# Windowed attention and an expert layer on one core: the second product of the last two chunks in seven products for eight

## The chip, the core and the metric

One of the eight cores of a Trainium2 chip runs one program. Its engines work side by side, each in the order of its own program: TensorE (PE; its weight loads are shown as PEld), VectorE (DVE), ScalarE (ACT), GpSimd (POOL), and SyncE (SP), which issues nearly all DMAs here. The metric is the device time of one execution in microseconds (us). Lower is better.

## The reference, cut to what matters

```python
scores = scale * q @ k.T                   # 8 x 8 heads, 576 positions, 64 wide; half the heads with a
attn = softmax(where(mask, scores, -1e9))  # window of 32, half with a dilated one
x = (attn @ v) as [4608, 512]
h = x @ w_in                               # w_in 512 x 2048
sp = maximum(h, 0) + log1p(exp(-abs(h)))   # softplus
g = h * erf(sp)
out = g @ w_out                            # w_out 2048 x 512
```

The inputs are float32 (the weights reach the chip as the bits of float64). A product of two float32 matrices is made of three TensorE products: each operand is split into a high part, which TensorE's fp32r format holds, and a low part, the rest; hi*hi + hi*lo + lo*hi is summed in PSUM.

## The kernel before

**Chunks.** The 4608 tokens are nine chunks of 512. The attention is worked off in small units between the matmuls of the first chunks, and its output x is kept turned, features on partitions. Three chunks (`PAIRED`) go through both products in the plain way: `mm1` (line 511) makes h, `mm2` (line 630) multiplies g with w_out. The other six are three pairs (`DOUBLES`), and the h of a pair is made by Strassen's algorithm: seven products for eight over two halves of the 512 features, two halves of a block d of 256 hidden columns, and the two chunks A and B. The sums of x (`big_load`, `big_less`, `big_hi`, `big_lo`) and of w_in (`build`, kept in DRAM as `ws`) are made ahead; `load_left` (line 576) brings the seven left operands of each d, in two DMAs.

**One d of a pair.** `mm1_big(d, k)` (761) is product k, six matmuls of 128x128 by 128x512 into one of two PSUM banks, `h` and `tx`. `take_big(d, k)` (771) adds it on VectorE to the sums that become h of A and of B, 128x1024 each. `argument_big` (798) is softplus on ScalarE: for A after take 4, for B after take 6. Erf needs another table of ScalarE; it runs in the next period (877), then `multiply_big` (803) makes g on VectorE. The g of B is stored to DRAM (`kept_g`), and `load_g` (810) brings it back when its turn comes; the g of A stays in SBUF.

**Periods.** `period(i, late)` (837) writes out the order of the work. Each period multiplies one item, the g of one chunk for one d, with w_out: 24 matmuls of 128x128 by 128x512 (`item_products`, 821; `mm`, 635), in four quarters of six, into four accumulators of 512 tokens by 512 columns. `split_item` (817) cuts g into its parts one period ahead. Eight of a pair's sixteen periods also hold the 42 matmuls of an h, in four groups between the quarters. So the items run behind h: with the last pair, d=16 to 23, periods 32 and 33 still multiply the last g of the pair before, periods 34 to 39 start the pair's A, and ten more periods without h end the program with the last of A and all of B.

**Order.** Nothing is rearranged: under `manual_schedule` every engine has its instructions in the order in which the code emits them, and waits on semaphores for what it needs. SP is one queue too. `AFT` lists small jobs by period and quarter, among them those that prepare the next pair. A tile name has a fixed number of buffers (`rows` 4, `w` 4, `hc`, `s`, `ghi`, `glo` 2, `v0`, `v1`, `qk0`, `qk1`, `o` 1); who takes one waits until its last readers are done, DMAs among them.

Of the kernel before, what the change touches and what calls it, by code (L numbers as in the profile page):

```python
# [139 lines left out]
def attn_moe_kernel(ctx: ExitStack, tc: tile.TileContext, qk, v, masks, eye, w_in, w_out, out):  # L140
# [518 lines left out]
    def store(c):  # L659
        last = c == NCH - 1  # L660
        for tt in range(TOK // P):
# [83 lines left out]
    for k in range(1, DOUBLES):  # L745
# [14 lines left out]

    def mm1_big(d, k):
        bank_ = (h, bank)[(7 * d + k) % 2]
        name = ORDER[k]
        w = left(NT + d).rearrange("p (b i c n) -> p b i c n", b=len(LEFT), i=2, c=2)[:, LEFT.index(name)]
        x = big[RIGHT[LEFT.index(name)]]
        for c in range(2):
            for n, (wi, xi) in enumerate(((0, 0), (0, 1), (1, 0))):
                nc.tensor.matmul(bank_, w[:, wi, c, :], x[c][:, xi, :],  # L768
                                 start=(c == 0 and n == 0), stop=(c == 1 and n == 2))

    def take_big(d, k):
        y = (h, bank)[(7 * d + k) % 2]
        if k == 0:
# [2 lines left out]
        add = lambda out, to: nc.vector.tensor_tensor(out=out, in0=y, in1=to, op=ALU.add)  # L776
        if k == 0:
            nc.vector.tensor_copy(out=a[:, 1], in_=y)  # L778
        elif k == 1:
            add(a[:, 0], a[:, 1])  # L780
        elif k == 2:
            add(b[:, 0], a[:, 1])
        elif k == 3:
            add(b[:, 1], b[:, 0])
        elif k == 4:
            add(a[:, 1], b[:, 1])
        elif k == 5:
            nc.vector.tensor_tensor(out=b, in0=y.rearrange("p (j n) -> p j n", j=1).broadcast_to([P, PAIR, TOK]),
                                    in1=b, op=ALU.add)
# [13 lines left out]
    def multiply_big(kind_, d):  # L803
        e = hs[kind_, d]
        nc.vector.tensor_tensor(out=e, in0=e, in1=ls[kind_, d], op=ALU.mult)
# [319 lines left out]
```

## Time and profile before

| | |
|---|---|
| three runs | 892.3, 893.34, 897.2 us, median 893.34 |
| the profiled execution | 892.89 us, span 890.9 us |
| busy, of the span | PE 871.2, PEld 700.1, DVE 633.6, ACT 564.5, POOL 81.3 us |
| first product of d=18 | at 743.06 us |
| last matmul | starts at 886.99 us |

The profile shows one execution. A row of a group of instructions has the line, engine, operation, what it writes<-reads, the shape, the count, then busy time and mean ns of one, and the idle time ahead of it with what ended it. A row of the timeline or of the chain of waits has its start and its length in us first; equal neighbours are merged (x6). Matmuls overlap in the pipeline, so one lasts longer than the step from start to start.

### The profile page before, as it was taken

To read this page: it belongs to the slowest core of one execution; us is meant where nothing else is said; L and a number is where in the kernel's file an instruction comes from. 1 tells how busy PE (TensorE), PEld (TensorE's weight loads), DVE (VectorE), ACT (ScalarE), POOL (GpSimd) and SP (SyncE) were. 2 spreads that over 40 slices of the span, in tenths; PEclk is the share of its full clock that TensorE was granted. 3 is DMA by queue.
4 is the path that set the end of the run, shared out by engine and by line. 5 is a ranking of instruction groups with operands and counts; after the bars stand their busy time and mean duration, and the time that the engine had idled before them with its cause. 6 is when DMAs were issued, how large, how long until landed. Compare 5 with 4: busy or idle time off the path is not lost.

```text
span 890.9 us, 20870 instructions
## 1 busy us (share of the span) xinstructions
PE 871.2 (98%) x8134; PEld 700.1 (79%) x8134; DVE 633.6 (71%) x1575; ACT 564.5 (63%) x1271; POOL 81.3 (9%) x97
## 2 busy tenths in 40 slices
PE   7799999999999999999999999999999999999998
PEld 3367888888888888788887778888888888888886
DVE  5878888987798889777676765666566647576622
ACT  6889888897788886675677442774445434445321
POOL 2312201111111110011000000010000000000000
PEclk9999999999999999999999999999999999999999
DMA  8874446464658896566675741674449125442341
GB/s 272 295 245 154 128 155 197 148 232 127 222 203 270 295 341 248 172 224 221 204 239 200 272 176 54 209 237 161 166 155 361 51 83 200 166 154 83 140 144 48
DMA packets 66915, 170.41 MB, mean 191 GB/s; under 512 B 7680, under 2 KB 14592, under 8 KB 63744
## 3 DMA queue, kind: packets, MB, share of 16 engines
q1 hardware_dynamic: 66528, 168.55, 55.1%
q8 instruction: 64, 1.05, 0.5%
q10 hardware_dynamic: 288, 0.52, 0.2%
q14 instruction: 35, 0.29, 0.1%
HBM read 122.91 MB, written 46.14 MB: 190 GB/s over the span
## 4 chain that ended last, share of the span: by engine, by line
PE 91%; DVE 5%; DMA 1%; ACT 1%; issue 1%; POOL 1%; SPq 0%; DVEq 0%; POOLq 0%; ACTq 0%
PE acc L636 43%; PE h L768 13%; PE tx L768 13%; PE h L521 7%; PE tx L521 7%; PE sp L275 3%; PE sp L217 3%; PE sp L256 1%; PE h L357 1%; DMA qk<-in_qk_dram 1%; DMA v<-in_v_dram 1%; DVE w L458 0%; DVE w L459 0%; DVE prob L228 0%; DVE win L453 0%
## 5 line engine op out<-in xcount | busy, mean ns | idle before, releaser
L636 PE MATMUL acc<-wout_hi,ghi 128*128 128x512 f32 x576 | 227.4, 395 | 0.5 <-DVE ghi L611 0.4
L636 PE MATMUL acc<-wout_lo,ghi 128*128 128x512 f32 x576 | 224.6, 390 | 0.0
L636 PE MATMUL acc<-wout_hi,glo 128*128 128x512 f32 x576 | 159.0, 389 | 0.0
L636 PEld LDWEIGHTS acc<-wout_hi,ghi 128*128 128x128 f32 x576 | 108.2, 188 | 23.3 <-DVE ghi L611 0.9
L636 PEld LDWEIGHTS acc<-wout_hi,glo 128*128 128x128 f32 x576 | 108.1, 188 | 22.8
L636 PEld LDWEIGHTS acc<-wout_lo,ghi 128*128 128x128 f32 x576 | 108.2, 188 | 21.7
L251 POOL TENSOR_TENSOR prob<-prob,rinv 128x256 f32<-128x256 f32 x72 | 72.7, 1016 | 477.0 <-DVE ssum L249 239.9
L238 ACT ACTIVATE prob<-prob,nmax 128x64 f32<-128x64 f32 x288 | 96.3, 338 | 10.5 <-DVE nmax L228 10.3
L801 ACT ACT_TABLE_LOAD x24 | 30.8, 1283 | 93.0 <-DVE dbl L776 47.3
L768 PE MATMUL tx<-win 128*128 128x512 f32 x288 | 74.1, 392 | 0.8 <-DVE hc L778 0.8
L228 DVE CUSTOM_DVE_ANT_0 prob<-sp,cst 128x64 f32<-128x64 f32 x288 | 45.3, 220 | 40.6 <-ACT rows L317 28.2
L768 PE MATMUL h<-win 128*128 128x512 f32 x288 | 74.0, 392 | 0.0
L768 PEld LDWEIGHTS tx<-win 128*128 128x128 f32 x288 | 53.5, 188 | 12.7 <-DVE hc L778 1.2
L768 PEld LDWEIGHTS h<-win 128*128 128x128 f32 x288 | 53.4, 188 | 12.0 <-DVE dbl L778 0.8
L612 DVE TENSOR_TENSOR glo<-hc,ghi 128x512 fp32r<-128x512 f32 x50 | 34.5, 692 | 33.4 <-PE acc L636 22.6
L238 ACT ACTIVATION_READ_ACCUMULATOR prob<-prob,nmax 128x1 f32 x288 | 54.7, 190 | 0.0
L612 DVE TENSOR_TENSOR glo<-dbl,ghi 128x512 fp32r<-128x512 f32 x48 | 33.4, 696 | 28.3 <-PE acc L636 15.6
L521 PE MATMUL h<-x,win 128*128 128x512 f32 x192 | 48.8, 396 | 0.0
L877 ACT ACTIVATE s<-s 128x1024 f32<-128x1024 f32 x48 | 48.2, 1052 | 0.3
L521 PE MATMUL tx<-x,win 128*128 128x512 f32 x192 | 48.0, 392 | 0.0
L801 ACT ACTIVATE s<-hc 128x1024 f32<-128x1024 f32 x24 | 25.5, 1061 | 34.9 <-DVE hc L776 22.8
L611 ACT CAST ghi<-hc 128x512 fp32r<-128x512 f32 x24 | 14.9, 623 | 50.0 <-PE acc L636 41.9
(146 smaller groups left out, 1519.7 us busy)
## 6 DMA issues: line engine op xcount, KB each, us to landing
win<-ws SPq DMA_DIRECT2D x24, 1024.0 KB, 5.0
v<-in_v_dram SPq DMA_DIRECT2D x72, 256.0 KB, 4.9
win<-ws SPq DMA_DIRECT2D x24, 768.0 KB, 5.1
qk<-in_qk_dram SPq DMA_DIRECT2D x48, 272.0 KB, 4.8
dbl<-in_w_in_dram SPq DMA_DIRECT2D x16, 512.0 KB, 4.4
dbl<-in_w_out_dram SPq DMA_DIRECT2D x16, 512.0 KB, 3.9
ws<-x SPq DMA_DIRECT2D x32, 256.0 KB, 4.3
qk<-in_qk_dram SPq DMA_DIRECT2D x24, 288.0 KB, 4.3
```

Source lines behind the costliest of these rows:

```text
L217: nc.tensor.matmul(sps[h][r * STRIP:(r + 1) * STRIP, i, p, :], qkz[i][hs, s * STRIP:(s + 1) * STRIP], qkz[i][hs, at:at + KEYS], start=True ...
L228: nc.vector.tensor_tensor_reduce(out=pr[:, g, :], in0=sps[h][:, u % 2, p, :], in1=mask[QUADS.index(kinds(u, p))], scale=-SCALE, scalar=HUG ...
L238: nc.scalar.activation(out=probs[u][:, j, :], in_=probs[u][:, j, :], func=AF.Exp, scale=-1.0, bias=nmax[:, j:j + 1], accum_out=sums[u][:, ...
L251: nc.gpsimd.tensor_tensor(probs[u], probs[u], rinv.broadcast_to([P, 2 * PARTS, KEYS]), op=ALU.mult)
L275: nc.tensor.matmul(xp[h * D:(h + 1) * D, qs], vt[ks, s, h, :], pt[ks, h * P + s * STRIP:h * P + (s + 1) * STRIP], start=True, stop=True, t ...
L521: nc.tensor.matmul((h, bank)[j], win_at[:, ftp, j, cc // 2, w, cc % 2, :], x[cc], start=(k == 0 and i == 0), stop=(k == CC - 1 and i == 2))
L611: (copy or nc.vector.tensor_copy)(out=ghi, in_=e)
L612: nc.vector.tensor_tensor(out=glo, in0=e, in1=ghi.bitcast(F32), op=ALU.subtract)
L636: nc.tensor.matmul(args["out"], args["lhsT"], args["rhs"], start=args["start"], stop=args["stop"])
L768: nc.tensor.matmul(bank_, w[:, wi, c, :], x[c][:, xi, :], start=(c == 0 and n == 0), stop=(c == 1 and n == 2))
L801: nc.scalar.activation(out=ls[kind_, d], in_=hs[kind_, d], func=AF.Softplus)
L877: nc.scalar.activation(out=e, in_=e, func=AF.Erf)
```

## The change

The second product of the last pair (`FIN`, d=16 to 23) is taken out of the periods and done at the end, by Strassen's algorithm, and the last h are done before it without items between.

- `ITEMS` ends with the second pair. Periods 32 and 33 stay; `final(d)` does d=18 to 23: the 42 matmuls of h, takes, softplus, erf of d-1 and its g, in four PSUM banks (`bank_of`) for two. The g of A is now stored to DRAM too.
- Products of w_out's blocks need sums of blocks. `sub_sums(p)` makes them for 256 rows of w_out on GpSimd from high plus low part (two adds of 128x512, four subtractions of 128x256), `sub_split(p)` splits them on ScalarE and VectorE and stores them to DRAM (`wd`), `load_sums(p)` brings them back into cells of `win` that h no longer needs. Eight p: the first five in periods 24 to 33, the others behind `final`.
- At the end `sums_step(s)` runs 16 times: chunk A or B, half of its 512 tokens, quarter q of the hidden columns. A step has seven products of six matmuls of 128x128 by 128x256, and the four steps of a half sum up in seven of the eight PSUM banks. `load_e` brings 256 tokens of g for two d, `row_sums` makes four sums of its blocks (four VectorE operations of 128x256), `operands` the high parts on ScalarE and the low parts on VectorE, two steps ahead. In each fourth step `sums_out` puts the seven products together and stores the result.

```diff
+FIN = DOUBLES - 1
+QUART = SPC // 2
+LASTS = [(kind_, half, q) for kind_ in "AB" for half in range(2) for q in range(QUART)]
...
-    kept_g = [dram.tile([SPC, P, PAIR, TOK], F32, name=f"g{i}") for i in range(DOUBLES)]
+    kept_g = {("B", i): dram.tile([SPC, P, PAIR, TOK], F32, name=f"g{i}") for i in range(DOUBLES)}
+    kept_g["A", FIN] = dram.tile([SPC, P, PAIR, TOK], F32, name="ga")
...
+    i = 2 * SPC * FIN
+    for p, at_ in enumerate((i - 8, i - 6, i - 4, i - 2, i)):
+        also(at_, 0, (lambda p: sub_sums(p), p))
+        also(at_ + 1, 3, (lambda p: sub_split(p), p))
+    also(i + 1, 3, (lambda p: sub_sums(p), 5))
...
-    ITEMS = [NT - 2, NT - 1] + [(kind_, i * SPC + k) for i in range(DOUBLES) for kind_ in "AB" for k in range(SPC)]
+    ITEMS = [NT - 2, NT - 1] + [(kind_, i * SPC + k) for i in range(FIN) for kind_ in "AB" for k in range(SPC)]
+
+    def bank_of(d, k):
+        return (h, bank, *spb)[(7 * d + k) % (4 if d >= FIN * SPC else 2)]
...
-        if kind_ == "B":
-            nc.sync.dma_start(out=kept_g[d // SPC][d % SPC], in_=e)
+        if (kind_, d // SPC) in kept_g:
+            nc.sync.dma_start(out=kept_g[kind_, d // SPC][d % SPC], in_=e)
...
+    def sub_sums(p):
+        r = subs[p] = [work.tile([P, S], F32, name="rows", bufs=4)[:, 0:TOK] for _ in range(2)]
+        for j in range(2):
+            less(r[j], wout_hi[:, 2 * p + j, :].bitcast(F32), wout_lo[:, 2 * p + j, :].bitcast(F32), ALU.add, nc.gpsimd)
+        (b11, b12), (b21, b22) = [(t[:, 0:HN], t[:, HN:TOK]) for t in r]
+        less(b11, b12, b11, engine=nc.gpsimd)
...
+    def sub_split(p):
+        tag = ("v", "qk")[p % 2]
+        for j, r in enumerate(subs.pop(p)):
+            hi = one.tile([P, QW + KW if p % 2 else TOK], F32R, name=f"{tag}{j}")[:, 0:TOK]
+            nc.scalar.copy(out=hi, in_=r)
+            less(r.bitcast(F32R), r, hi.bitcast(F32))
+            for i, t in enumerate((hi.bitcast(F32), r)):
+                nc.sync.dma_start(out=wd[p][:, j, i], in_=t)
...
+    def load_sums(p):
+        for j, c in enumerate(ROOM[p]):
+            nc.sync.dma_start(out=cell(c).bitcast(F32), in_=wd[p][:, j])
...
+    def op_room(s):
+        if s % 2 == 0:
+            return [work.tile([P, S], F32R, name="rows", bufs=4)[:, 0:TOK] for _ in range(4)] + [
+                one.tile([P, QW + KW], F32R, name=f"qk{i}")[:, 0:TOK] for i in range(2)] + [
+                one.tile([P, TOK], F32R, name="v0")]
...
+    def sums_product(s, k):
+        q = s % QUART
+        y, (xh, xl) = bank_at(s, k), operand(s, k)
+        for j in range(2):
+            at_, (wh, wl) = slice(j * P, (j + 1) * P), right(2 * q + j)[k]
+            for n, (x, w) in enumerate(((xh, wh), (xh, wl), (xl, wh))):
+                nc.tensor.matmul(y, x[:, at_], w, start=(q == 0 and j == 0 and n == 0),
+                                 stop=(q == QUART - 1 and j == 1 and n == 2))
...
+    def final(d):
+        k0 = d - FIN * SPC
+        mm1_big(d, 0)
+        mm1_big(d, 1)
+        for kind_ in "AB":
+            e = ls[kind_, d - 1]
+            nc.scalar.activation(out=e, in_=e, func=AF.Erf)
+        take_big(d, 0)
+        take_big(d, 1)
+        multiply_big("A", d - 1)
+        for k in (2, 3):
+            mm1_big(d, k)
+            take_big(d, k)
+        multiply_big("B", d - 1)
+        load_left(NT + d + 2, 0)
+        mm1_big(d, 4)
+        take_big(d, 4)
+        argument_big("A", d)
+        mm1_big(d, 5)
+        mm1_big(d, 6)
+        take_big(d, 5)
+        take_big(d, 6)
+        argument_big("B", d)
+        load_left(NT + d + 2, 1)
+        jobs(LATE.get(k0, ()))
...
+    LATE = {2: [(sub_split, 5), (sub_sums, 6), (load_e, 0, room_w)],
+            3: [(sub_split, 6), (sub_sums, 7), (row_sums, 0, room_w)],
+            4: [(sub_split, 7), (operands_all, 0), (load_e, 1, room_w)],
+            5: [(row_sums, 1, room_w)],
+            6: [(load_sums, 0), (load_sums, 1), (operands_all, 1)],
+            7: [(load_sums, 2), (load_sums, 3), (load_e, 2, lambda: slab(0)), (load_sums, 4), (load_sums, 5)]}
+
+    def sums_step(s):
+        last_ = s % QUART == QUART - 1
+        for g, ks in enumerate(GROUPS):
+            for k in ks:
+                sums_product(s, k)
+            if s == 0 and g == 0:
+                d = DOUBLES * SPC - 1
+                for kind_ in "AB":
+                    nc.scalar.activation(out=ls[kind_, d], in_=ls[kind_, d], func=AF.Erf)
+                for kind_ in "AB":
+                    multiply_big(kind_, d)
+                load_e(3, lambda: room_e(3))
+                load_sums(6)
+                load_sums(7)
+            if g == 0:
+                row_sums(s + 2, room_s)
+            if last_:
+                for k in ks:
+                    sums_out(s, k)
+            operands(s + 2, g)
+        load_e(s + 4, lambda: room_e(s + 4))
...
+        for d in range(FIN * SPC + 2, DOUBLES * SPC):
+            final(d)
+        for s in range(len(LASTS)):
+            sums_step(s)
```

More of the change, by code (lines that the diff above doesn't have):

```diff
@@ new lines, in sum_at, with right, load_e @@
+    def sum_at(p, j, n):
+        return [cell(ROOM[p][j])[:, i, n * HN:(n + 1) * HN] for i in range(2)]
+    def right(p):
+        w11, w12, w21, w22 = ([w[:, 2 * p + j, n * HN:(n + 1) * HN] for w in (wout_hi, wout_lo)]
+                              for j in range(2) for n in range(2))
+        return w11, w21, sum_at(p, 1, 1), sum_at(p, 0, 1), sum_at(p, 0, 0), w22, sum_at(p, 1, 0)
+    es, rs, ops = {}, {}, {}
+    GROUPS = ((0, 1), (2, 3), (4, 5), (6,))
+    def load_e(s, room):
+        if s < len(LASTS):
+            kind_, half, q = LASTS[s]
+            es[s] = room()
+            for k in range(2):
+                to = es[s][k] if isinstance(es[s], list) else es[s][:, k]
+                nc.sync.dma_start(out=to.rearrange("p (j n) -> p j n", j=PAIR),
+                                  in_=kept_g[kind_, FIN][2 * q + k][:, :, half * HN:(half + 1) * HN])
@@ new lines, in room_s @@
+    def room_s():
+        t = work.tile([P, PAIR, TOK], F32, name="s")
+        return [t[:, 0], t[:, 1]]
+    def op_room(s):
[3 more added lines that the diff above has]
+                one.tile([P, TOK], F32R, name="v0")]
+        return [work.tile([P, TOK], F32R, name=n) for n in ("ghi", "glo", "ghi", "glo")] + [
+            one.tile([P, TOK], F32R, name="v1"), one.tile([P, TOK], F32R, name="pT1"),
+            small.tile([P, DM], F32R, name="o", bufs=1)]
@@ new lines, in operands @@
+    def operands(s, g):
+        if s >= len(LASTS):
+            return
+        if g == 0:
+            ops[s] = op_room(s)
+        room = ops[s]
+        if g == 3:
+            hi, lo = room[6][:, 0:HN], room[6][:, HN:TOK]
+            at_ = lambda t, ks: t.rearrange("p (k n) -> p k n", k=2)[:, ks]
+            src = [(ks, e[:, :, 1, 1, :]) for ks, e in parts_of(s)]
+        elif g:
+            hi, lo = room[2 * g:2 * g + 2]
+            at_ = lambda t, ks: t
+            src = [(None, rs[s][g - 1])]
+        else:
+            hi, lo = room[0:2]
+            at_ = lambda t, ks: t.rearrange("p (j k n) -> p j k n", j=PAIR, k=2)[:, :, ks]
+            src = [(ks, e[:, :, :, 0, :].rearrange("p k j n -> p j k n")) for ks, e in parts_of(s)]
+        for ks, t in src:
+            nc.scalar.copy(out=at_(hi, ks), in_=t)
+        for ks, t in src:
+            less(at_(lo, ks), t, at_(hi, ks).bitcast(F32))
@@ new lines, in attn_moe_kernel, with sums_out, put @@
+    kept_u = {}
+    def sums_out(s, k):
+        y, r0 = bank_at(s, k), (NCH - 2) * TOK + s // QUART * HN
+        new = lambda: io.tile([P, TOK], F32, name="w", bufs=4)[:, 0:HN]
+        def put(t, r, n):
+            nc.sync.dma_start(out=out[r0 + r * P:r0 + (r + 1) * P, n * HN:(n + 1) * HN], in_=t)
+        u = kept_u
+        if k == 0:
+            u[0] = new()
+            nc.scalar.copy(out=u[0], in_=y)
+        elif k == 1:
+            t = new()
+            less(t, y, u[0], ALU.add)
+            put(t, 0, 0)
+        elif k == 2:
+            less(u[0], y, u[0], ALU.add)
+        elif k == 3:
+            u[1] = new()
+            less(u[1], y, u[0], ALU.add)
+        elif k == 4:
+            t = new()
+            less(t, y, u[1], ALU.add)
+            put(t, 1, 1)
+            less(u[0], y, u[0], ALU.add)
+        elif k == 5:
+            less(u[0], y, u[0], ALU.add)
+            put(u[0], 0, 1)
+        else:
+            less(u[1], u[1], y)
+            put(u[1], 1, 0)
@@ new lines, in operands_all @@
+    def operands_all(s):
+        for g in range(4):
+            operands(s, g)
+    LATE = {2: [(sub_split, 5), (sub_sums, 6), (load_e, 0, room_w)],
[4 more added lines that the diff above has]
+            7: [(load_sums, 2), (load_sums, 3), (load_e, 2, lambda: slab(0)), (load_sums, 4), (load_sums, 5)]}
```

46 lines of the change are left out of this document (43 added, 3 removed).

## The prediction

> **What bounds the kernel now.** I read the page first: span, busy shares, the chain that ended last.
>
> ```profile
> span 890.9 us, 20870 instructions
> PE 871.2 (98%) x8134; PEld 700.1 (79%) x8134; DVE 633.6 (71%) x1575; ACT 564.5 (63%) x1271; POOL 81.3 (9%) x97
> PE 91%; DVE 5%; DMA 1%; ACT 1%; issue 1%; POOL 1%; SPq 0%; DVEq 0%; POOLq 0%; ACTq 0%
> GB/s 272 295 245 154 128 155 197 148 232 127 222 203 270 295 341 248 172 224 221 204 239 200 272 176 54 209 237 161 166 155 361 51 83 200 166 154 83 140 144 48
> ```
>
> TensorE is the bound over the whole span. A share is an average, so next I cut out the stretch that the change rewrites, by windows (busy time of PE, PEld, DVE, ACT, POOL; clock; DMA share; GB/s), and took the end of the chain in order of time.
>
> ```profile
> 669.60:713.00 43.40, 43.40 (x193) 35.93 (x192) 28.47 (x44) 21.17 (x34) 0.00 (x0) 1.00 0.56 200
> 743.06:887.00 143.94, 143.94 (x637) 119.18 (x635) 77.78 (x108) 56.78 (x61) 0.00 (x0) 1.00 0.37 128
> 830.26 57.13 PE acc L636 x252
> ```
>
> At 743.06 the first product of d=18 starts; up to 887.0 PE never stops, at full clock. The stretch holds 6x42=252 matmuls of h and 16x24=384 of the second product. One step is 57.13/252 = 0.2267 us. VectorE (77.78 of 143.94) and ScalarE (56.78) have air. Here a saved matmul is saved time only while the other engines keep up with the faster order.
>
> **The matmuls.** Removed: 384x0.2267 = 87.05 us. Added: 16 steps of 7x6 = 672 matmuls of 256 columns, each with its own weight load. The trace has no 128x256 matmul, so I bound it by the timeline's nearest rows.
>
> ```profile
> 5.05 1.47 PE L357 MATMUL h<-plain 128*128 128x512 bf16 x6
> 6.84 0.60 PE L357 MATMUL h<-plain 128*128 128x512 bf16 x2
> 236.14 0.60 PE L256 MATMUL sp<-ident,prob 128*128 128x128 f32 x4
> 236.46 0.19 PEld L636 LDWEIGHTS acc<-wout_hi,ghi 128*128 128x128 f32 x1
> 236.57 0.19 PEld L636 LDWEIGHTS acc<-wout_lo,ghi 128*128 128x128 f32 x1
> ```
>
> Four more bf16 matmuls of 512 columns take 1.47-0.60 = 0.87, 0.2175 each; the fp32r ones take 0.2267. So some 0.009 us is paid per matmul and not per column: half the columns save about 0.109, leaving 0.118. If all of it were per column it would be 0.113. The other limit is the weight load: two follow each other after 0.11 us, and four transposes, each with a load, come every (0.60-0.27)/3 = 0.11 (0.27 being one's duration). I take 0.120, near the first estimate; bounds 0.11 and 0.125, and 0.19 if a load's whole recorded time had to pass between two matmuls. 672x0.120 = 80.6: **gain 6.4 us** (13.1 at 0.11, 3.0 at 0.125, a loss of 40.6 at 0.19). Seven for eight is 12.5%, but what a matmul costs beside its columns is paid 672 times, not 384.
>
> The Trainium skill (TensorE: Matmul & The Clock Gate, Back-to-back issue gap) states N/2.4 + 2.5 ns warm, 109 ns for 256 columns. The bf16 rows agree with it (216 ns for 512), the fp32r ones here are 11 ns longer; by the page alone the gain would be 13.8 us.
>
> **h without cover.** Before, each d had its 42 matmuls of h mixed with 24 of an item, 66x0.2267 = 14.96 us; now d=18 to 23 have 9.52 us each, with nothing between. The round through ScalarE and VectorE stays. Its rows, from the timeline:
>
> ```profile
> 753.13 0.68 DVE L776 TENSOR_TENSOR dbl<-h,dbl 128x512 f32<-128x512 f32 x1
> 753.89 1.28 ACT L801 ACT_TABLE_LOAD   x1 [5.86 <-DVE dbl L776]
> 755.18 1.06 ACT L801 ACTIVATE s<-dbl 128x1024 f32<-128x1024 f32 x1
> 754.14 1.23 DVE L788 TENSOR_TENSOR dbl<-tx,dbl 128x1024 f32<-128x1024 f32 x1 [0.33 <-PE tx L768]
> 758.73 1.28 ACT L877 ACT_TABLE_LOAD   x1
> 760.02 2.01 ACT L877 ACTIVATE s<-s 128x1024 f32<-128x1024 f32 x2
> 755.28 1.22 DVE L805 TENSOR_TENSOR hc<-hc,s 128x1024 f32<-128x1024 f32 x1
> L729 ACT CAST win<-w 128x512 fp32r<-128x512 f32 x12 | 7.0, 616 | 0.6 <-DVE w L716 0.6
> L260 ACT COPY pT<-acc 128x256 f32<-128x256 f32 x7 | 2.6, 366 | 0.0
> L733 DVE TENSOR_TENSOR win<-w,win 128x512 fp32r<-128x512 f32 x12 | 7.6, 684 | 0.0
> 327.44 0.42 DVE L540 TENSOR_TENSOR plain<-plain 128x256 f32<-128x256 f32 x1
> 327.90 0.42 DVE L541 TENSOR_TENSOR plain<-plain 128x256 f32<-128x256 f32 x1
> ```
>
> From take 4 of d to take 4 of d+1, in final()'s order: softplus table 1.29, softplus A and B 0.96 each (two ACTIVATEs take 2.01, so the second starts 0.96 after the first), erf table 1.29, erf A 1.05; then on VectorE multiply A 1.14 (starts follow each other some 0.08 before the recorded end), takes 2 and 3 0.61 each, multiply B 1.14, take 4 0.69; three handovers of 0.1. Sum 10.0 us against 9.52. Takes 2 to 4 stand behind multiply A, PE waits for their banks. Four banks give three products, 4.1 us, once. Six rounds are 60.0 against 57.1: +2.9.
>
> Into this round come, ahead of the erf table in ScalarE's order: two 128x512 copies (0.616, 0.52 from start to start) of sub_split behind d=17 to 20, 4x1.04 = 4.2; operands_all(0) and (1), each two whole copies, and g 0 and 3 in two halves of 256 and 128 columns (about 0.28 and 0.2), 2.0 a time, 4.1. On VectorE behind d=19: the two subtractions (0.61 each) and eight row sums of 128 columns (some 0.32 each: 0.46 a step at 256) with takes 0 and 1 are 5.1 us where ScalarE keeps it 4.3: +0.8. The other row sums hide behind ScalarE's tables.
>
> One wait is new: operands(0) writes the four `rows` buffers and `qk0`, `qk1`, and sub_split(7), just ahead, stores from them to DRAM. ScalarE's copy of group 1 must wait until those stores have landed, behind both parts of load_left for d=22 on the one queue SP.
>
> ```profile
> win<-ws SPq DMA_DIRECT2D x24, 1024.0 KB, 5.0
> g<-dbl SPq DMA_DIRECT2D x12, 512.0 KB, 2.9
> ```
>
> Alone a 512 KB store lands in 2.9 us; 1792 KB ahead of it take 5.1 at 361 GB/s, the best slice of the page. Bounds 1 and 7; I take 4. Queued behind that copy: erf A and B of d=20, so multiply A, so takes 2 to 6, so PE.
> Sum for h: 2.9+4.2+4.1+0.8+4 = **+16.0** (bounds: the bare round, 3, and 20).
>
> **Into the sums.** load_sums(2) to (5) and e2 stand on SP behind the store of B(22), which waits for multiply B(22), by then as late as PE's end of h. From there until step 3 can run its third product, the queue must move 4 MiB of sums, e2 and e3, three stores of g, and sums 6 and 7, which stand behind e3, which waits until A(23) is stored: 8.5 MiB, 24.7 us at 361 GB/s. PE would be there after 3x5.04+1.44 = 16.6. Lag 8.1, and about 1 for the store's landing: **+9** (1 if the loads of sums 2 to 5 go out as soon as their cells are free, 14 with a round trip more).
>
> **Hidden, or nothing.** Per step of 5.04 us VectorE has four row sums (1.6) and three and a half low parts (2.2), and every fourth step eight adds out of PSUM at 0.34 to 0.46: 4.5 on average, so it keeps up, at 90%; operands are built two steps ahead. ScalarE has 1.9. GpSimd's two whole and four half sums per p:
>
> ```profile
> 313.91 0.61 POOL L251 TENSOR_TENSOR prob<-prob,rinv 128x256 f32<-128x256 f32 x1 [6.96 <-DVE rinv L250]
> 314.09 0.72 DVE L541 TENSOR_TENSOR dbl<-dbl 128x256 f32<-128x256 f32 x1
> ```
>
> 0.61 for 128x256, so 2x1.2+4x0.61 = 4.9 us per p, and VectorE beside it went from 0.42 to 0.72. In the stretch without h VectorE has 14.9 us of 43.40 free; four p there bring 5.5 of subtractions and 24x0.3 = 7.2 of such delays: hidden by 2 us, up to +3 if not. The end: one add of 0.42 in place of a copy of 0.59: -0.2.
>
> The Trainium skill (SBUF — State Buffer, Who interferes with whom) says the port pair that VectorE and GpSimd share is an exclusive lock and the later one blocks; 0.72 for 0.42 agrees. By it a whole sum could hold VectorE 1.2 us.
>
> **Sum.** The profiled execution took 892.89 us (the median of the three runs is 893.34): 892.9-6.4+16.0+9.0-0.2 = 911.3.
>
> **Rivals.**
> - *All cover holds*, and only matmuls count: 892.9-6.6 = 886.3, 880 at 0.11. For it: full banks, operands two steps ahead. The point that decides: the round from take 4 to take 4, copies included, must average under 9.52+4.1/6 = 10.2 us; I add up 10.0 bare and 12 with the copies. **Faster**, 0.14.
> - *Only the round counts*: the loads are in time and the `rows` wait is short: 892.9-6.4+12 = 898; with half the copies fitting into gaps 893. 0.18, half of it within 0.5%.
> - *Weight loads show*: 0.19 a matmul: 892.9+40.6+16 = 949; the loads then come in time. Against it: 0.11 between two loads. 0.05.
> - *GpSimd holds VectorE for its whole time*, not 0.3 an op: in the periods without h 4x4.9 = 19.6 and 5.5 stand against 14.9 free, +10: 921. Against it: 0.42 became 0.72 beside a 0.61. 0.05.
>
> **How the numbers follow.** The forecast has 0.58. 0.5% is 4.5 us, about what a measurement of this kernel can tell. Faster 0.14; same 0.09; slower 0.77. Low end: the round's 3 and 1 for the loads, 892.9-6.4+3+1 = 890.5, rounded down; high end: 0.125 a matmul, 20 and 14: 924. Range 889 to 924, likeliest 911; its own range is 902 to 922.
>
> **What would show it.** Steady steps of 42 matmuls: 5.04 us. h: 42 matmuls of d=20 to 23 in 10 to 14 us, PE idle ahead of product 4 to 6, released by takes 0 to 2; the longest idle ahead of d=21 or 22, with ScalarE's L-line of operands waiting for a DMA. Steps 1 to 4: PE waiting for DMA. I am wrong if PE stays without gaps from d=18 on, or if a step takes over 5.5 us.

## The result, and the profile after

The changed kernel takes 927.11 us (median of 5 runs, 926.18 to 927.47). On the same chip the kernel before takes 893.81 us (5 runs, 892.3 to 897.2). The ratio is 1.0367, with a 95% interval of 1.0345 to 1.0390: slower by 33 us. The forecast was 911 us, slower, with a range that ended at 924.

The page of the changed kernel: its span, the busy shares, the granted clock and the traffic in 40 slices, and the chain that ended last.

```profile
span 925.3 us, 21992 instructions
PE 878.9 (95%) x8410; PEld 719.7 (78%) x8422; DVE 697.5 (75%) x1707; ACT 595.4 (64%) x1339; POOL 132.7 (14%) x145
PEclk9899999999999999999999999999998999798999
GB/s 276 285 247 138 143 152 176 213 190 90 241 245 313 277 325 181 182 273 209 187 240 240 222 46 198 238 158 160 187 335 157 125 255 358 262 259 330 160 122 63
PE 82%; DMA 6%; DVE 6%; ACT 3%; issue 2%; POOL 0%; DVEq 0%; ACTq 0%; SPq 0%; POOLq 0%
```

TensorE's share of the chain has fallen from 91% to 82%; DMA has gone from 1% to 6%. Late in the span there are slices with a lower clock. I cut the end of the span into its three stages by windows: the periods up to the first product of d=18, the h of d=18 to 23, and the sixteen steps (busy time of PE, PEld, DVE, ACT, POOL; clock; DMA share; GB/s). The row of the first stage in the kernel before stands behind them.

```profile
640.00:750.96 110.96, 106.97 (x455) 87.28 (x454) 79.91 (x98) 48.63 (x65) 27.97 (x24) 0.97 0.56 193
750.96:825.74 74.78, 62.44 (x253) 49.84 (x252) 57.38 (x89) 46.29 (x56) 11.93 (x12) 0.91 0.83 302
825.74:921.98 96.24, 86.85 (x672) 84.91 (x671) 66.18 (x145) 37.56 (x66) 0.00 (x0) 0.95 0.52 177
```

```profile
640.00:743.06 103.06, 103.06 (x456) 85.33 (x455) 64.26 (x92) 44.77 (x57) 0.00 (x0) 1.00 0.46 162
```

Against the kernel before, span against span (890.94 to 925.25):

| stage | before | after | difference | in the prediction |
|---|---|---|---|---|
| up to d=18 | 743.06 | 750.96 | +7.9 | 0 |
| h of d=18 to 23 | 57.12 (6x9.52) | 74.78 | +17.7 | +16.0 |
| second product, 87.05 before | 87.05 | 96.24 | +9.2 | -6.4+9.0 = +2.6 |
| behind the last matmul | 3.95 | 3.27 | -0.7 | -0.2 |

The four add up to +34.1 of 34.3. The prediction had 18.4. The difference lies in the first row and the third. (A round is one d of h without items between, from take 4 to take 4; the lag is what the sixteen steps take beyond their matmuls.)

**The periods.** In the timeline around TensorE's two pauses of this stage, VectorE, GpSimd and PE in turn; a bracket tells how long the engine had been idle and what released it:

```profile
690.00 1.78 DVE L722 TENSOR_TENSOR w<-plain,o 128x512 f32<-128x512 f32 x1
691.70 2.93 DVE L739 TENSOR_TENSOR win<-win 128x512 fp32r<-128x512 f32 x2
694.56 2.37 DVE L948 TENSOR_TENSOR rows<-rows,qk 128x512 fp32r<-128x512 f32 x2
696.85 1.81 DVE L617 TENSOR_TENSOR glo<-hc,ghi 128x512 fp32r<-128x512 f32 x2
...
689.58 3.36 POOL L948 TENSOR_TENSOR rows<-wout_hi,wout_lo 128x512 f32<-128x512 f32 x2 [68.48 <-DVE glo L617]
692.90 4.62 POOL L948 TENSOR_TENSOR rows<-rows 128x256 f32<-128x256 f32 x4
...
698.11 1.71 PE L641 MATMUL acc<-wout_hi,glo 128*128 128x512 f32 x4 [1.96 <-DVE glo L617]
711.13 0.50 PE L641 MATMUL acc<-wout_hi,ghi 128*128 128x512 f32 x1 [2.03 <-ACT ghi L616]
```

While GpSimd makes the sums of one p (7.9 us), two subtractions of VectorE take 2.93 us; TensorE then waits 1.96 us for a low part that stands behind them.

**The h.** The rows of the rounds of d=20 and d=21, VectorE's, ScalarE's and PE's:

```profile
776.17 1.94 DVE L948 TENSOR_TENSOR rows<-rows,v 128x512 fp32r<-128x512 f32 x2 [1.85 <-ACT v L966]
778.03 1.94 DVE L948 TENSOR_TENSOR w<-w 128x128 f32<-128x128 f32 x8
796.68 0.69 DVE L948 TENSOR_TENSOR rows<-w,rows 128x512 fp32r<-128x512 f32 x1 [5.12 <-DMA wd<-rows]
...
795.39 0.62 ACT L1055 CAST rows<-w 128x512 fp32r<-128x512 f32 x1 [4.74 <-DMA wd<-rows]
...
780.62 2.93 PE L786 MATMUL h<-x,win 128*128 128x512 f32 x6 [3.62 <-DVE dbl L796]
799.04 1.22 PE L786 MATMUL sp<-x,win 128*128 128x512 f32 x2 [7.04 <-DVE hc L796]
```

The longest idle time of TensorE, 7.04 us in d=21, goes back to the operands' copy on ScalarE, which waits 4.74 us for the stores of the sums. The low parts of the same operands wait with it on VectorE, and take 0 of d=21, for which TensorE waits, stands behind them. The second, 3.62 us in d=20, was not in the prediction in this form: the subtractions of a split wait 1.85 us for ScalarE's copies behind two softplus, and the row sums and takes 0 and 1 stand behind them on VectorE. Six matmuls take 2.93 us there in place of 1.52, at half the clock.

**The steps.** The chain of waits through the first four steps, and then the group of these loads on the page:

```profile
825.90 1.15 PE acc L1078 x10
827.05 6.62 DMA win<-wd
833.74 10.46 DMA win<-wd
844.24 1.33 PE acc L1078 x9
847.70 7.61 DMA win<-wd
```

```profile
win<-wd SPq DMA_DIRECT2D x16, 512.0 KB, 6.9
```

Steps 0 to 4 take 5.03, 11.29, 7.09, 11.02 and 6.60 us; from step 5 on every step takes 5.03 us, the last 4.91 to its last matmul's start. So the lag is 96.24-80.6 = 15.6 us, where I had 9.

**The clock.** Windows laid on the stretches in which matmuls last twice as long (same columns as above):

```profile
698.60:702.00 3.40, 3.40 (x10) 2.61 (x9) 3.40 (x5) 0.17 (x1) 2.01 (x2) 0.50 1.00 310
712.20:715.60 3.40, 3.40 (x10) 2.66 (x9) 3.40 (x5) 0.62 (x1) 1.58 (x2) 0.50 1.00 313
794.20:804.40 10.20, 5.36 (x13) 4.20 (x14) 7.15 (x11) 5.11 (x8) 0.00 (x0) 0.50 0.42 154
835.10:841.90 6.80, 5.69 (x26) 5.70 (x27) 3.66 (x8) 2.06 (x4) 0.00 (x0) 0.50 1.04 358
```

The clock is halved behind pauses, for 3.4 us or a multiple of it. Summed over the matmuls (start to start, above their 0.227 and 0.120 us) this is about 3 us in the periods, 4 in h and 4 in the steps, some 11 us together; where a pause ends and slow matmuls begin is a choice, so these are no exact numbers. Whether that is time lost is a question for an experiment.

### The profile page after: what moved, and what is told of

Same layout as the page of the kernel before. It is cut to its first block, busy times and chain, and to the rows that moved or that the text cites. A ratio compares the mean times of both kernels' runs of the same rounds, so it can differ in the third digit from the quotient of the medians.

```text
span 925.3 us, 21992 instructions
## 1 busy us (share of the span) xinstructions
PE 878.9 (95%) x8410; PEld 719.7 (78%) x8422; DVE 697.5 (75%) x1707; ACT 595.4 (64%) x1339; POOL 132.7 (14%) x145
## 4 chain that ended last, share of the span: by engine, by line
PE 82%; DMA 6%; DVE 6%; ACT 3%; issue 2%; POOL 0%; DVEq 0%; ACTq 0%; SPq 0%; POOLq 0%
PE acc L641 32%; PE tx L786 9%; PE h L786 9%; PE tx L526 7%; PE h L526 7%; PE acc L1078 4%; PE sp L280 3%; PE sp L222 3%; DMA win<-wd 3%; PE sp L786 2%; DMA qk<-in_qk_dram 2%; PE sp L1078 2%; PE sp L261 1%; PE h L1078 1%; PE tx L1078 1%
## 5 line engine op out<-in xcount | busy, mean ns | idle before, releaser
L641 PE MATMUL acc<-wout_hi,ghi 128*128 128x512 f32 x448 | 178.9, 399 | 2.5 <-ACT ghi L616 2.0
L641 PE MATMUL acc<-wout_lo,ghi 128*128 128x512 f32 x448 | 175.9, 393 | 0.0
L641 PE MATMUL acc<-wout_hi,glo 128*128 128x512 f32 x448 | 125.3, 393 | 2.0 <-DVE glo L617 2.0
L641 PEld LDWEIGHTS acc<-wout_hi,ghi 128*128 128x128 f32 x448 | 85.0, 190 | 20.7 <-ACT ghi L616 2.9
L641 PEld LDWEIGHTS acc<-wout_hi,glo 128*128 128x128 f32 x448 | 84.7, 189 | 20.5 <-DVE glo L617 2.4
L641 PEld LDWEIGHTS acc<-wout_lo,ghi 128*128 128x128 f32 x448 | 84.9, 190 | 16.9
L322 ACT COPY rows<-sp 128x128 f32<-128x128 f32 (+7 forms) x167 | 27.5, 307 | 27.6 <-PE sp L222 27.6
L526 PEld LDWEIGHTS tx<-x,win 128*128 128x128 f32 x192 | 36.8, 194 | 7.8
L526 PEld LDWEIGHTS h<-x,win 128*128 128x128 f32 x192 | 35.4, 188 | 8.0
L819 ACT ACTIVATE s<-dbl 128x1024 f32<-128x1024 f32 x24 | 25.1, 1058 | 24.2 <-DVE dbl L794 24.1
```

What stands on the lines that cost most here:

```text
L322: nc.scalar.copy(out=to, in_=src)
L526: nc.tensor.matmul((h, bank)[j], win_at[:, ftp, j, cc // 2, w, cc % 2, :], x[cc], start=(k == 0 and i == 0), stop=(k == CC - 1 and i == 2))
L641: nc.tensor.matmul(args["out"], args["lhsT"], args["rhs"], start=args["start"], stop=args["stop"])
L819: nc.scalar.activation(out=ls[kind_, d], in_=hs[kind_, d], func=AF.Softplus)
```

## The experiments

Each kernel is run against the kernel before on the same chip (893.0 to 893.8 us there). The theory after the result: (1) the sums on GpSimd slow VectorE in the periods, about 8 us; (2) the splits and the `rows` wait hold the rounds of h; (3) the loads of the sums fill the DMA queue behind h. Stages are read as above.

| run | whole, us | ratio, 95% | d=18 at | h | steps |
|---|---|---|---|---|---|
| the change | 927.11 | 1.0345 to 1.0390 | 750.96 | 74.78 | 96.24 |
| e1_other_room | 919.80 | 1.0269 to 1.0319 | 749.93 | 71.17 | 93.03 |
| e2_no_gpsimd | 916.35 | 1.0230 to 1.0281 | 742.88 | 73.04 | 94.70 |
| e3_sums_early | 920.41 | 1.0269 to 1.0315 | 757.86 | 62.39 | 95.95 |
| e4_no_loads | 915.86 | 1.0226 to 1.0274 | 749.28 | 76.16 | 84.28 |
| e5_vector_sums | 915.89 | 1.0247 to 1.0284 | 752.00 | 64.41 | 93.29 |
| e6_filled_waits | 928.24 | 1.0375 to 1.0417 | 749.11 | 76.81 | 97.04 |
| e7_load_order | 925.16 | 1.0341 to 1.0382 | 750.98 | 76.15 | 93.13 |
| e8_bare_h | 914.89 | 1.0226 to 1.0267 | 752.20 | 64.83 | 93.21 |
| e9_half_bytes | 920.93 | 1.0285 to 1.0334 | 748.58 | 74.41 | 89.61 |
| e10_ceiling | 891.16 | 0.9962 to 0.9989 | 741.74 | 62.22 | 80.35 |
| e11_memset | 917.71 | 1.0249 to 1.0293 | 743.01 | 74.65 | 95.88 |
| e12_round_short | 914.06 | 1.0207 to 1.0249 | 753.96 | 61.59 | 93.15 |

### The wait on `rows`: e1_other_room

```diff
 def op_room(s):
-        if s % 2 == 0:
+        if s % 2 == 1:
```

> The changed kernel with the two rooms of the operands exchanged: steps 0, 2, ... take ghi, glo, v1, pT1 and o, steps 1, 3, ... take the rows buffers, qk0, qk1 and v0. Nothing else differs. Theory (the copy of group 1 behind d=20 waits for the stores of the sums of w_out out of the same buffers, 4.7 us, and PE goes to half clock over it): the gap of PE in d=21 shrinks from 7.4 to about 3 us, d=21 from 19.4 to about 14 us, the whole to 919 to 922. Rival (that wait hides behind the round through ScalarE and VectorE, which is late anyway): d=21 stays above 17 us, the whole at 926 to 928.

919.8 us, 7.3 less. The operands of step 0 now go to other buffers, and ScalarE's copies come without a wait behind those of the split (timeline):

```profile
788.30 1.12 ACT L966 CAST qk<-rows 128x512 fp32r<-128x512 f32 x2
789.33 1.23 ACT L1055 CAST ghi<-w 128x256 fp32r<-128x256 f32 x3
```

d=21 takes 11.12 us in place of 19.35. 4.6 us of these 8.2 come back in other rounds: d=23 takes 13.70 in place of 10.48, d=20 16.25 in place of 14.99. The steps, on the other hand, are 3.2 us shorter; why is not followed up here. The wait that the prediction named is real.

### GpSimd in the periods: e2_no_gpsimd, e11_memset

e2 leaves out the instructions on GpSimd; the split reads w_out's high part in their place:

```diff
 def sub_sums(p):
...
-            less(r[j], wout_hi[:, 2 * p + j, :].bitcast(F32), wout_lo[:, 2 * p + j, :].bitcast(F32), ALU.add, nc.gpsimd)
-        (b11, b12), (b21, b22) = [(t[:, 0:HN], t[:, HN:TOK]) for t in r]
-        less(b11, b12, b11, engine=nc.gpsimd)
...
+        subs[p] = [wout_hi[:, 2 * p + j, :].bitcast(F32) for j in range(2)]
```

> The eight sums on GpSimd are left out: the high part of w_out is split in their place, with the same copies, subtractions and stores. The output is not the reference's. Theory (GpSimd and VectorE hold each other up in the two gaps of PE ahead of h and behind d=19): the first product of d=18 comes at about 745 instead of 751 us, d=20 falls from 15.0 to about 13 us, the whole to 917 to 920. Rival (the added copies and subtractions themselves, standing in the order of ScalarE and VectorE ahead of the parts of g, make those gaps): d=18 stays at 749 to 751, the whole at 925 to 927.

The first product of d=18 starts at 742.88 us, 0.2 us from the kernel before. The 8 us of the periods belong to GpSimd's sums; the splits, which stay, cost nothing there. The size is less sharp than one profile makes it: in the change and in the five runs below that share its code up to d=18 (e1, e4, e6, e7, e9) d=18 starts between 748.58 and 750.98, so the cost is 5.6 to 8 us. d=20 takes 14.55 us and d=21 18.38, little less than the 14.99 and 19.35 of the change, where 13 were expected of d=20: there GpSimd is not the main cause.

e11 asks what it is in GpSimd's work, its mere presence, its lateness or its reads:

```diff
 def sub_sums(p):
...
-        for j in range(2):
-            less(r[j], wout_hi[:, 2 * p + j, :].bitcast(F32), wout_lo[:, 2 * p + j, :].bitcast(F32), ALU.add, nc.gpsimd)
...
+        for n in range(10):
+            nc.gpsimd.memset(r[n % 2], 1.0)
```

> This is the changed kernel with the ten reading instructions of each sum of w_out on GpSimd (about 12 us together beside VectorE) replaced by ten memsets of 128x512, which write and read nothing (the output is not the reference's); buffers, splits, stores and loads stand. Theory, that VectorE's own instructions are slowed by GpSimd's reads of SBUF beside them: first product of d=18 at 743 to 744 us, as in the run without GpSimd (742.9), the whole at 916 to 919 us. Rival, that ScalarE's copies and the splits wait for a late GpSimd, or that any work of GpSimd on SBUF slows VectorE: d=18 at 748 us or later, the whole at 922 us or more.

d=18 starts at 743.01 us and the whole takes 917.7, as the theory had it. GpSimd is busy in both (27.97 us in the change's periods, 19.26 here), the buffers and splits are the same, and VectorE's row has the same 98 instructions:

```profile
640.00:743.01 103.01, 103.01 (x455) 85.08 (x454) 67.56 (x98) 48.63 (x65) 19.26 (x40) 1.00 0.60 208
```

67.56 us of VectorE against 79.91 in the change, and 67.50 in e2, where GpSimd does nothing in this stretch: memsets add nothing to the same 98 instructions; the sums, which read, add 12.35 us. The groups by line and form, of the change and then of e11, show it in one operation:

```profile
L739 DVE TENSOR_TENSOR win<-win 128x512 fp32r<-128x512 f32 x4 | 5.3, 1364 | 0.0
L948 POOL TENSOR_TENSOR rows<-rows 128x256 f32<-128x256 f32 x16 | 16.1, 1006 | 0.9
L948 POOL TENSOR_TENSOR rows<-wout_hi,wout_lo 128x512 f32<-128x512 f32 x8 | 12.0, 1509 | 81.7 <-DVE glo L617 68.5 <-DMA wd<-rows 13.2
```

```profile
L739 DVE TENSOR_TENSOR win<-win 128x512 fp32r<-128x512 f32 x4 | 2.6, 680 | 0.0
L954 POOL MEMSET rows<- 128x512 f32 x50 | 24.1, 530 | 118.0 <-DMA wd<-rows 118.0
```

Beside memsets a subtraction takes 680 ns, beside the sums 1364. The Trainium skill (SBUF — State Buffer, Who interferes with whom) says that a VectorE instruction with two inputs in SBUF contends with a GpSimd instruction that reads SBUF, and not with one that only writes it. These two runs agree.

### The sums elsewhere: e3_sums_early, e5_vector_sums

e3 keeps them on GpSimd, but does all eight p in periods 20 to 24, where the second pair's h comes to its end, and none beside the h of d=18 to 23:

```diff
-    for p, at_ in enumerate((i - 8, i - 6, i - 4, i - 2, i)):
-        also(at_, 0, (lambda p: sub_sums(p), p))
...
+    SUMS_AT = ((-12, 3), (-11, 0), (-11, 2), (-10, 0), (-10, 2), (-9, 0), (-9, 1), (-9, 3))
+    SPLIT_AT = ((-11, 1), (-11, 2), (-10, 0), (-10, 2), (-9, 0), (-9, 2), (-9, 3), (-8, 3))
...
-    LATE = {2: [(sub_split, 5), (sub_sums, 6), (load_e, 0, room_w)],
+    LATE = {2: [(load_e, 0, room_w)],
```

> All eight sums of w_out are made, split and stored in periods 20 to 24, beside h of the second pair, where a period lasts 15 us; final() has no sums left, only e0, e1 and the operands of steps 0 and 1. Theory (the crowd in the short periods costs 8 us with the half clock, and the copies, the GpSimd sums and the rows wait cost h some 11): d=18 starts at 743 to 744, h takes 63 to 66 us instead of 74.8 (the bare round of 10.0 us six times, and the operands), the steps 94 to 97 as before, the whole 906 to 910. Rival (the round is bound by takes and tables alone, so h stays long): h 72 us or more, the whole 917 or more.

h falls to 62.39 us, so the sums, their splits and their wait cost it 12.4. But d=18 starts 6.9 us later still, and the whole is 920.4, not the 906 to 910 expected: I had taken VectorE's free time in these periods as an average once more. The window over them, and PE's two long waits:

```profile
646.00:690.00 44.00, 35.71 (x143) 28.57 (x142) 37.04 (x39) 20.81 (x25) 32.92 (x29) 0.88 0.80 266
657.06 1.20 PE L789 MATMUL h<-dbl,win 128*128 128x512 f32 x3 [2.88 <-DVE dbl L797]
684.76 0.79 PE L641 MATMUL acc<-wout_hi,ghi 128*128 128x512 f32 x1 [5.41 <-DVE ghi L616]
```

e5 puts them on VectorE, in three portions, and spreads them over periods 20 to 25, 32 and 33, none in `final`. It also issues the loads of sums 2, 3 and 6 earlier, which e7 below does alone:

```diff
-            less(r[j], wout_hi[:, 2 * p + j, :].bitcast(F32), wout_lo[:, 2 * p + j, :].bitcast(F32), ALU.add, nc.gpsimd)
...
+            less(r[j], wout_hi[:, 2 * p + j, :].bitcast(F32), wout_lo[:, 2 * p + j, :].bitcast(F32), ALU.add)
...
+    for n, (at_, q) in enumerate(SLOTS):
+        also(at_, q, (lambda n: (sub_sums, sub_less, sub_split)[n % 3](n // 3), n))
```

> All eight sums of w_out are made on VectorE instead of GpSimd, in three chunks of 1.3 to 1.5 us per p (two adds; four subtractions; the split) spread over the quarters of periods 20 to 25, 32 and 33; final() has none; the loads of sums 2 and 3 go out inside d=23 as soon as their cells are free, and sums 6 ahead of e3. Theory (VectorE alone pays 2.8 us per p where GpSimd beside it cost more through the shared port): d=18 starts at 743 to 745, h 62 to 63 us as with the early sums on GpSimd, the steps 88 to 91, the whole 898 to 904. Rival (with two banks PE waits for VectorE whoever brings the extra work): d=18 at 748 or later, the whole 906 or more. On the change as such both say: not below the kernel before.

915.9 us, with d=18 at 752.0: the rival was right. In the window VectorE is busy 79.57 of 102 us and TensorE is idle for 6.66 us (102.00-95.34), in four pauses above all, of which one is shown:

```profile
640.00:742.00 102.00, 95.34 (x412) 76.37 (x411) 79.57 (x130) 48.33 (x66) 0.00 (x0) 1.00 0.63 216
661.21 1.66 PE L786 MATMUL tx<-win 128*128 128x512 f32 x6 [2.04 <-DVE hc L796]
```

Whoever makes the sums, in these periods VectorE's order had no room for them where they were put, although its share says so.

### The loads: e4_no_loads, e7_load_order, e9_half_bytes

e4 leaves out the loads of sums 2 to 7.

```diff
-            7: [(load_sums, 2), (load_sums, 3), (load_e, 2, lambda: slab(0)), (load_sums, 4), (load_sums, 5)]}
+            7: [(load_e, 2, lambda: slab(0))]}
...
-                load_sums(6)
-                load_sums(7)
```

> The loads of the sums 2 to 7 are left out (6 MiB), the products of steps 1 to 3 read what lies in those cells. The output is not the reference's. Theory (steps 0 to 4 wait for the one DMA queue): 16 steps take 81 to 84 us instead of 96.4, the waits of PE there nearly vanish and the half clock with them, the whole 912 to 915. Rival (g of d=23 comes late through ScalarE and VectorE, and steps 2 and 3 wait for their operands): steps 90 us or more, the whole 921 or more.

The steps take 84.28 us, 12.0 less, and the whole 11.3 less. The same window over the first steps in the change and in e4:

```profile
826.00:862.00 36.00, 27.21 (x180) 25.64 (x178) 17.32 (x34) 13.67 (x21) 0.00 (x0) 0.86 0.84 292
826.00:846.00 20.00, 16.53 (x113) 15.95 (x112) 8.67 (x14) 8.64 (x10) 0.00 (x0) 0.83 0.92 327
```

```profile
826.00:862.00 36.00, 33.60 (x270) 32.42 (x269) 26.89 (x57) 17.83 (x29) 0.00 (x0) 1.00 0.52 172
```

270 matmuls against 180 in 36 us. The 84.28 us are still 3.7 above 80.6: in steps 2 to 4 of e4 TensorE waits 0.78, 1.03 and 0.48 us for sums and low parts on VectorE. e7 keeps all loads, with sums 2 and 3 issued at the beginning of d=23 and sums 6 ahead of e3:

```diff
+        if d == DOUBLES * SPC - 1:
+            load_sums(2)
+            load_sums(3)
...
+                load_sums(6)
                 load_e(3, lambda: room_e(3))
-                load_sums(6)
```

> The changed kernel, but the loads of sums 2 and 3 stand on SP inside d=23, ahead of the stores of g of d=22, and sums 6 ahead of e3. Theory (their place on SP, behind stores that wait for VectorE and for a landing, makes half of the lag of steps 0 to 4): steps 88 to 92 instead of 96.2, the whole 919 to 923. Rival (the 8.5 MiB themselves take the time, in whatever order): steps 94 or more, the whole 925 or more.

The steps take 93.13 us, 3.1 less: the order is worth a fifth of the lag, between what theory and rival expected. h takes 1.4 us more (76.15), so the whole gains only 2.0, to 925.2. e9 leaves all loads at their places and halves each:

```diff
 def load_sums(p):
...
-            nc.sync.dma_start(out=cell(c).bitcast(F32), in_=wd[p][:, j])
+            nc.sync.dma_start(out=cell(c).bitcast(F32)[:, 0], in_=wd[p][:, j, 0])
```

> This is the changed kernel with each of the 16 loads of a sum of w_out cut to its high part, 256 KB in place of 512 KB (the products with a low part read what lies in the cell, so the output is not the reference's); the number of loads, their order and every wait stand. The sixteen steps took 96.2 us with all bytes and 84.3 without the loads of sums 2 to 7. Theory, that the bytes in the queue set the lag: steps of 88 to 91 us, the whole at 919 to 922 us. Rival, that the order of the loads and what each issue waits for on its queue set it: steps of 94 us or more, the whole at 925 us or more.

89.61 us, close to the middle of 96.24 and 84.28, which is 90.3. The profiled execution is the fastest of the four (917.64 us, the others 920.4 to 921.46); by the medians of the whole, half the bytes gain 6.2 us where e4 gains 11.3. Both say that this part of the lag follows the bytes.

### The clock: e6_filled_waits

Matmuls whose result nobody reads are put into the waits of d=20 and 21 and of steps 1 and 3, so that TensorE stands still there for a shorter time:

```diff
+    def fill(y, n):
+        for _ in range(n):
+            nc.tensor.matmul(y, wout_hi[:, 0, 0:P], wout_hi[:, 1, :], start=True, stop=True)
...
+            fill(acc[3], {FIN * SPC + 4: 14, FIN * SPC + 5: 30}.get(d, 0))
...
+            fill(BANKS[(7 - s // QUART) % len(BANKS)], {(1, 1): 12, (3, 0): 8, (3, 1): 12}.get((s, g), 0))
```

> The changed kernel with matmuls that nobody reads, 128x128 by 128x512 into a bank that is free, put where PE waits: 14 ahead of product 4 of d=20, 30 ahead of product 4 of d=21, 12 ahead of the third product of steps 1 and 3, 8 ahead of step 3. Each lot is a little shorter than the wait it stands in. Theory (the granted clock falls to half for 3.4 us and more after each long wait, and this costs 3.8 us in h and 4.6 in the steps): the mean clock from d=18 on rises to nearly 1, h 71 to 73, steps 91 to 94, the whole 919 to 922. Rival (what PE loses at half clock is waited for anyway): the whole 926 to 928.

928.2 us, no gain, though the half-clock loss falls from some 11 to some 6 us. Ahead of product 4 of d=20 the fill does what it is there for: the six matmuls behind it take 1.66 us in place of 2.93. What comes next waits all the longer. In the change ScalarE's copy is released at 795.39; here, from the timeline:

```profile
795.44 0.62 ACT L1055 CAST rows<-w 128x512 fp32r<-128x512 f32 x1 [6.36 <-DMA wd<-rows]
```

The copy waits 1.6 us longer for the same moment, the end of a transfer, and d=22 starts at 805.90 (805.74 in the change). In the steps the last wait for a load ends 30.1 us behind the first product, in the change 29.6. So at the filled waits of d=20 and of the steps the half clock cost nothing of its own: what is made faster ahead of the next wait is waited for. In d=21 the fill did not keep the clock up: 3.43 us of idle time are left there and the six matmuls behind it take 2.93 us as in the change. For this wait, and for the two pauses in the periods, which e6 leaves, it is not shown whether the half clock costs time.

### The bare round: e8_bare_h, e12_round_short

e8 is e5 with the row sums and operands of steps 0 and 1 behind d=23, so that the rounds of d=19 to 22 hold nothing of the change:

```diff
-            3: [(row_sums, 0, room_w)],
-            4: [(operands_all, 0), (load_e, 1, room_w)],
-            5: [(row_sums, 1, room_w)],
-            6: [(load_sums, 0), (load_sums, 1), (operands_all, 1)],
+            6: [(load_sums, 0), (load_sums, 1)],
+            7: [(row_sums, 0, room_w), (operands_all, 0), (load_e, 1, room_w), (row_sums, 1, room_w), (operands_all, 1),
...
```

> As the kernel with the sums on VectorE, but the row sums and operands of steps 0 and 1 are made behind d=23 and no longer inside h: final() has nothing but h, takes, tables and g. The steps start later for it, so only h is compared. If the bare round of 10.0 us binds and four banks give 4.1 us once, six rounds cost 60.0-57.1=2.9, which the banks can just pay: h 57 to 58 us. Rival one (the banks are used up already, every round costs its half microsecond): h 59.5 to 60.5. Rival two (GpSimd was the cause in the earlier runs, and the round is far from binding): 57.1 flat, with VectorE and ScalarE idle over 15% of it.

ScalarE's softplus tables in the timeline come in a steady period:

```profile
762.67 1.28 ACT L819 ACT_TABLE_LOAD   x1 [4.58 <-DVE dbl L794]
772.81 1.28 ACT L819 ACT_TABLE_LOAD   x1 [3.52 <-DVE hc L794]
782.95 1.28 ACT L819 ACT_TABLE_LOAD   x1 [3.52 <-DVE dbl L794]
793.10 1.28 ACT L819 ACT_TABLE_LOAD   x1 [3.52 <-DVE hc L794]
```

10.14 us, where the prediction added up 10.0. What was moved behind d=23 is paid there: it takes 14.85 us, so h as a whole (64.83) can't be held against the three expectations. The other five d take 49.97 us, 10.0 each, as rival one had it: every round costs its half microsecond. e12 takes the multiplication of A out of the chain of the round:

```diff
-        multiply_big("A", d - 1)
         for k in (2, 3):
             mm1_big(d, k)
             take_big(d, k)
+        multiply_big("A", d - 1)
         multiply_big("B", d - 1)
```

> This is the kernel of the run with h bare, with the multiplication of the first chunk put behind the taking of products 2 and 3 in each round, so that the chain of a round (table load, two erf, the takings of products 0 to 3, then the argument) carries one instruction of VectorE less ahead of them. Theory, that this chain makes the round of 10.1 us: by the rows 1.3 us shorter, 8.8 us, below the product's 9.52 us, so that d=19 to 22 take 9.52 to 9.6 us each, h 62 to 63 us in place of 64.8, the whole at 912 to 913 us. Rival, that another chain (banks, the loads of the left operands, the table loads) makes it: rounds of 10.0 us or more, h of 64 us or more, the whole at 914 to 916 us.

d=20 to 22 take 9.52 us each, the products' own time (d=19 still 10.48), and h 61.59: the order on VectorE made the round. The whole gains less, 1.5 us from profile to profile and 0.8 by the medians. In this execution d=18 started 1.8 us later, with the same code up to there; one profile of these periods is no sharper than that.

### The ceiling: e10_ceiling

```diff
-    for p, at_ in enumerate((i - 8, i - 6, i - 4, i - 2, i)):
-        also(at_, 0, (lambda p: sub_sums(p), p))
-        also(at_ + 1, 3, (lambda p: sub_split(p), p))
...
 def operand(s, k):
-        room = ops[s]
+        room = ops[s % 2]
...
 def sums_step(s):
...
-            operands(s + 2, g)
-        load_e(s + 4, lambda: room_e(s + 4))
```

> This leaves out everything that the change adds to prepare its products: the sums of w_out, their splits, stores and loads, and the operands of all steps but the first two, which every later step reads again (so the output is not the reference's). What is left is h behind one another without other matmuls between, and 672 matmuls of 128x256. It shows what the change could give if all preparation were free. Theory by the terms: first product of d=18 at 743.0 us after the span's start as in the kernel before, h of 60 to 63 us (57.1 before, the bare round being longer than its product's 9.52 us), steps of 80.6 us (672 x 0.120), the whole at 889 to 893 us, so no more than 4 us below the kernel before. Rival, that h is delayed by the preparations alone and comes to 57.1 us without them: the whole at 884 to 887 us.

891.16 us, ratio 0.9962 to 0.9989. With nearly everything that prepares a product taken away (the operands of two steps stay, and every later step reads them again), the change is worth 2.5 us (893.67 to 891.16). Two windows, h and the steps:

```profile
741.74:803.96 62.22, 58.52 (x254) 46.83 (x253) 51.26 (x81) 41.94 (x48) 0.00 (x0) 1.00 0.72 262
803.96:884.30 80.34, 80.34 (x672) 80.34 (x671) 16.15 (x33) 8.07 (x10) 0.00 (x0) 1.00 0.11 42
```

The 672 matmuls take 80.34 us, 6.7 less than the 87.05 of before. h without cover takes 62.22, 5.1 more than 57.12; the operands of two steps are in it (d=18 to 20 take 9.52 us each, d=21 and d=23, behind these operands, 11.32 and 12.18). So the preparations cost the other 36 us (927.1-891.2).

## Why the prediction was right, and where it was wrong

**Right: the sign, the matmuls, the round, the `rows` wait.**
- *672x0.120 = 80.6*: measured 80.34 without waits, a steady step 5.03 against 5.04. By the formula of the Trainium skill alone (TensorE: Matmul & The Clock Gate, Back-to-back issue gap; 109 ns) an estimated 73.2; the measurement decides against it, 0.1196 us a matmul.
- *The bare round, 10.0 against 9.52*: 10.14 in e8, and e12 shows that it is the chain I summed, with multiply A ahead of takes 2 to 4.
- *The copy of operands that waits for the stores of sub_split(7), 4 us*: 4.74 measured; e1, which takes the cause away, takes 3.6 us off h and 7.3 off the whole. The way from there to TensorE was shorter than the one named: take 0 of d=21 stands behind the low parts of these operands on VectorE, and TensorE is released by it before erf of d=20 is done.
- *h, +16.0*: +17.7. Its parts stand less well than the sum. The bare round and the operands were 7.0 in the prediction and are 5.1 in e10; the splits and the `rows` wait were 9.0 and are 12.6 (74.78-62.22). I had costed a split by ScalarE's copies, with +0.8 for VectorE once. In the trace VectorE's subtractions wait 1.85 us for these copies each time, and the takes behind them on VectorE wait too: d=20 takes 14.99 us.

**Wrong: "hidden by 2 us, up to +3 if not", the sums on GpSimd in the periods.** They cost 7.9 us in the profiled execution (e2 and e11 give all of it back). Three sizes failed in this step. First GpSimd's time: I priced half a sum by one row, 0.61 us. The group of that operation on the page of before had the mean:

```profile
L251 POOL TENSOR_TENSOR prob<-prob,rinv 128x256 f32<-128x256 f32 x72 | 72.7, 1016 | 477.0 <-DVE ssum L249 239.9
```

1.0 us, which is what the sums took (1006 ns, and 1509 for a whole one), 7.0 us a p and not 4.9. The timeline of before shows why one row misled. Between 200 and 330 us the operation comes eighteen times: nine take 0.61 us, and nine 1.41, each of these begun while a 128x1024 instruction with two inputs was running on VectorE:

```profile
318.75 1.19 DVE L605 TENSOR_TENSOR s<-hc,s 128x1024 f32<-128x1024 f32 x1
319.00 1.41 POOL L251 TENSOR_TENSOR prob<-prob,rinv 128x256 f32<-128x256 f32 x1 [4.47 <-DVE rinv L250]
```

So in these rows the price went with what the other engine had begun, and that could be read before the change. Second VectorE's delays: 12.35 us for four p and not 7.2. Third, and this would have hurt with the right sizes too, I held them against 14.9 us free in the whole stretch of 43.40. VectorE works in order: in the rows shown it runs from 690.00 to 698.66 without a pause, and TensorE's low parts stand last in that row. The rival *GpSimd holds VectorE* had this mechanism at +10 us; it got a chance of 0.05 because its condition was read from the single 0.61 row.

**Wrong in size: "Lag 8.1, and about 1 for the store's landing", +9.** It is 15.6. e4 and e9 confirm the mechanism, bytes in the queue, for 12.0 of it. I let 8.5 MiB run at 361 GB/s, the best slice of a page; the trace has 327 over the first 20 us and 292 over 36. At 292 the same bytes take 30.5 us in place of 24.7, which is 5.8 of the 6.6 us missed. This split is worked out, not run, and it is no full account: e4 keeps 3.7 us of lag without these loads, in waits for VectorE, which the prediction had keep up. Order adds up to 3 us (e7).

**Not in the sum: the half clock.** Its 11 us or so must not simply be added as a term: e6 removed about 5 of them and gained nothing. What the rest costs, in d=21 above all, stays open.

Of the 15.9 us by which the sum fell short, 7.9 are GpSimd's, 6.6 the lag's, 1.7 those of h, and -0.5 the end's: 15.7. The range ended at 924 because its high end had 20 for h and 14 for the lag, but nothing for GpSimd.

What was to show it did: a step of 5.03 us, the longest idle time in d=21 behind a copy of ScalarE that waits for a DMA, TensorE waiting for DMAs in steps 1 to 4. Of d=20 to 23, said to take 10 to 14 us, d=20 and 21 lie above (14.99 and 19.35) and d=22 below (9.52). No pause had been named ahead of d=18.

## What to carry to other kernels

Ask first what a change is worth when all its preparation is free: here seven products for eight save 6.7 us of 87, h without cover takes 5.1 back, and 2.5 us were all that could be won before one prepared anything (e12's order of the round, which shortens h, was not tried with it). Cost a filler on a busy engine by the instructions that stand behind it in that engine's order, not by the engine's share over a stretch, and price an operation by the rows, or the mean of its group, in which the neighbour engine is at work. Price a queue of transfers by the rate that the trace sustains over such a stretch, not by its best slice.

## What the runs showed of the hardware that was not expected

- GpSimd's reads and writes differ for VectorE: beside memsets a 128x512 subtraction keeps 680 ns, beside sums that read two inputs it takes 1364 ns in the mean.
- The half clock comes after short pauses, but not after each. Behind pauses of 2.35 and 2.42 us (start to start) in the periods of the change there are 3.4 us at 0.50; in e5 a pause of 2.43 us is followed by full clock, and in e9 one of 3.15 us too; in e7 one of 3.15 us at the same place is followed by 6.8 us at 0.50. The Trainium skill (TensorE: Matmul & The Clock Gate, Why this matters for your kernels) has pauses over about 3 us lead back to the half clock; here shorter ones did, and of two of about that length one did and one did not.
